# Twin items of queries and keys on 128 partitions, a planned first phase, and fp32 transposes back

## The chip, the cores and the metric

The kernel runs on one core of a Trainium2 chip. The metric is the device time of one execution in microseconds (us). A profiled execution also has a span, from its first to its last instruction, which is some 1.8 us shorter than its time (457.6 and 459.36 us for the kernel before). All times of places inside the kernel are counted from the start of the span. Only one run of each kernel has its trace kept, so a place read from a trace is that of one execution.

Engines are named as the profile names them. PE is TensorE's matmuls and PEld its weight loads. DVE is VectorE, ACT is ScalarE, POOL is GpSimd, and SP is the engine that issues most transfers. SBUF and PSUM are the two memories in which the kernel lays its tiles, on up to 128 partitions. PE's results lie in PSUM.

## The reference

```python
# q, k, v: (8, 12, 448, 64) float32; tau = 0.1; w_in: (768, 2048); w_out: (2048, 768)
q_n = q / (norm(q, axis=-1, keepdims=True) + 1e-6)
k_n = k / (norm(k, axis=-1, keepdims=True) + 1e-6)
scores = q_n @ k_n.transpose(0, 1, 3, 2) / tau
attn = softmax(scores)                       # with 1e-9 in the denominator
x = (attn @ v).transpose(0, 2, 1, 3).reshape(3584, 768)
h = x @ w_in
g = h * clip(h + 3, 0, 6) / 6
out = g @ w_out
```

There are 96 heads, worked in 48 pairs, and six pairs make a batch. The first matrix product (`w_in`) of a batch needs all six of its pairs. The second (`w_out`) follows it.

## The kernel before

For each pair the queries and keys are loaded as float32, squared, summed, and scaled to bf16 unit vectors. PE transposes them and makes the scores, ACT takes the exps, and PE multiplies by the values. DVE divides by the sums, PE transposes back, and DVE copies the result to `xT`. Between these, "units" of the two matrix products of the batch before keep PE full: 16 units of the first product and 6 or 8 of the second per batch. In the first six pairs there are no units yet.

One load brings the queries of two pairs into all 128 partitions. The two heads of a pair lie on partitions 0 to 63 and 64 to 127. One transpose gives a pair's queries on 64 partitions and its keys on the others, and this kernel moves each on by copies of 64 partitions (five a pair, of 189 to 393 ns):

```python
    def load_qk(d, first=0, n_pairs=2, e0=nc.sync, e1=nc.sync):
        ...
        for n, (t, e) in enumerate(((q, e0), (k, e1))):
            e.dma_start(
                out=raw_of[d][:, first : first + n_pairs, n, :],
                in_=t[b, h : h + 2 * n_pairs].rearrange("(i g) (p c) d -> (g p) i (c d)", g=2, c=7),
            )
    ...
        copy(qT[lo, :], z[lo, :, 0, :])          # in transposes(): five copies of 64 partitions
        ...
    def back(i, bank):                           # the way back, in bf16
        for j in range(4):
            nc.tensor.transpose(Z[:, q_cols(b, j)], on[:, j, :, :], ident[:, :])
        nc.vector.tensor_copy(out=xT[...][:, hp, ...], in_=Z[:, 0:S])
```

The steady loop, from pair 6 on, issues units around the way back of the pair before:

```python
        n = 1 if i % HP == 0 else 2
        issue(us[:n])
        prepare(i, 2)
        if i > HP:
            back(i - 1, next_bank())
        issue(us[n:])
```

Six PSUM banks are shared by scores, transposes and units (the "ring" of `M0`, `M1`, `Y`, `Z`, `M2`, `M3`).

## Time and profile before

| | before |
|---|---|
| time, median of 3 runs | 458.64 us (458.5 to 459.07) |
| span of the profiled run, its clock | 457.6 us, 0.992 |
| first exp of pair 0 | 11.62 us |
| first scores of pair 6, the first with units | 37.91 us |
| first scores of pair 12, from where PE is full | 83.97 us |

Each digit is the busy share of one of 40 slices of 11.4 us, in tenths.

```profile
DMA  8999996505325144234244253244152001021022
```

### The profile page before, as it was taken

What the parts mean: (1) busy time and instruction counts of PE and PEld (TensorE: products, weight loads), DVE (VectorE), ACT (ScalarE), POOL (GpSimd) and SP (SyncE); (2) the same over time, 40 slices, a digit from 0 to 9 for tenths busy, and PEclk for the clock granted to TensorE, in tenths of its full rate; (3) what the DMA queues carried; (4) which work ended last, traced back from release to release, by engine and by line L of the source; (5) the groups of instructions that cost most, each with busy time, mean ns of one, the idle gap of its engine ahead of it and who ended that gap; (6) DMA issues with size and microseconds to landing.
All of it is one profiled execution on the core that took longest, in us unless ns stands there. A gap on an engine that the chain in (4) does not pass through costs nothing.

```text
span 457.6 us, 9825 instructions
## 1 busy us (share of the span) xinstructions
PE 432.5 (95%) x3872; PEld 260.5 (57%) x3872; DVE 277.0 (61%) x610; ACT 268.3 (59%) x584; POOL 187.2 (41%) x158
## 2 busy tenths in 40 slices
PE   1779799999999999999999999999999999999996
PEld 0455455556666666656666565656666566665553
DVE  6787487767654775775764766776674655414500
ACT  4797588567635665766754576576573657503410
POOL 4996865446144263364261561562460630000000
PEclk9999799999999999999999999999999999999999
DMA  8999996505325144234244253244152001021022
GB/s 279 222 246 259 250 214 173 145 13 157 112 63 172 23 135 140 72 103 139 64 109 144 51 157 111 62 139 129 31 155 52 19 19 36 19 69 36 1 72 69
DMA packets 41167, 50.98 MB, mean 111 GB/s; under 512 B 4256, under 2 KB 41120, under 8 KB 41120
## 3 DMA queue, kind: packets, MB, share of 16 engines
q1 hardware_dynamic: 35504, 43.50, 33.7%
q0 software_dynamic: 5248, 6.29, 8.2%
q8 instruction: 30, 0.49, 0.5%
q10 hardware_dynamic: 368, 0.56, 0.4%
q14 instruction: 17, 0.14, 0.1%
HBM read 45.61 MB, written 11.01 MB: 124 GB/s over the span
## 4 chain that ended last, share of the span: by engine, by line
PE 85%; ACT 5%; DVE 3%; issue 2%; DMA 2%; POOL 2%; SPq 0%; POOLq 0%; ACTq 0%; DVEq 0%
PE M L297 21%; PE M L323 20%; PE PV L258 9%; PE Y L323 6%; PE Z L297 5%; PE Z L323 5%; PE Y L297 5%; PE M L207 5%; ACT at L214 3%; PE M L170 2%; PE M L285 2%; DVE gT L308 1%; PE Y L207 1%; ACT u L305 1%; DMA vr<-in_v_dram 1%
## 5 line engine op out<-in xcount | busy, mean ns | idle before, releaser
L152 POOL TENSOR_TENSOR nrm<-raw,r 128x896 bf16<-128x896 f32 x47 | 79.3, 1688 | 184.1 <-ACT r L145 154.2
L323 PEld LDWEIGHTS <-gT 128*128 128x128 bf16 x896 | 87.3, 98 | 59.1 <-DVE gT L308 0.6
L214 ACT ACTIVATE at<-M 128x448 bf16<-128x448 f32 x197 | 94.8, 568 | 27.9 <-PE M L207 15.9
L297 PE MATMUL M<-xT,w_in_sb 128*128 128x448 bf16 x516 | 108.1, 355 | 0.0
L297 PEld LDWEIGHTS <-w_in_sb 128*128 128x128 bf16 x768 | 73.6, 98 | 59.0 <-issue 2.4
L323 PE MATMUL M<-w_out_sb,gT 128*128 128x384 bf16 x576 | 98.5, 326 | 0.2 <-DVE gT L308 0.2
L121 POOL TENSOR_TENSOR sq<-raw 128x896 f32<-128x896 f32 (+3 forms) x47 | 75.0, 1597 | 4.8 <-DMA raw<-in_k_dram 2.8
L308 DVE SCALAR_TENSOR_TENSOR gT<-u,M 128x448 bf16<-128x448 bf16 x86 | 52.5, 619 | 36.4 <-ACT u L305 36.1
L305 ACT ACTIVATE u<-M,half_bias 128x448 bf16<-128x448 f32 x86 | 53.9, 637 | 35.2 <-PE M L297 34.4
L258 PEld LDWEIGHTS <-at 128*128 128x128 bf16 x1344 | 54.1, 98 | 34.3 <-issue 23.4
L258 PE MATMUL PV<-vx,at 128*128 128x65 bf16 (+1 forms) x1344 | 65.2, 199 | 4.2 <-ACT at L214 3.6
L129 DVE TENSOR_REDUCE n<-sq 128x14 f32<-128x896 f32 x48 | 51.8, 1079 | 3.5 <-POOL sq L121 3.2
L207 PE MATMUL M<-qT,kz 64*128 64x448 bf16 (+1 forms) x197 | 41.9, 353 | 4.0 <-DVE gT L308 2.0
L348 ACT COPY o<-M 128x384 f32<-128x384 f32 x17 | 8.1, 478 | 48.3 <-PE M L323 48.3
L272 DVE RECIPROCAL rc<-PV 128x8 f32<-128x8 f32 x48 | 9.9, 206 | 41.4 <-PE PV L258 41.2
L170 PEld LDWEIGHTS <-nrm 128*128 128x128 bf16 x336 | 23.1, 101 | 20.8 <-DVE nrm L152 8.4
L273 DVE TENSOR_TENSOR on<-PV,rc 128x512 bf16<-128x512 f32 x48 | 33.2, 692 | 1.7
L214 ACT ACTIVATE at<-Z 128x448 bf16<-128x448 f32 x48 | 27.2, 566 | 11.2 <-PE M L207 10.9
L323 PE MATMUL Y<-w_out_sb,gT 128*128 128x384 bf16 x176 | 30.4, 326 | 0.0
L297 PE MATMUL Z<-xT,w_in_sb 128*128 128x448 bf16 x132 | 29.7, 363 | 0.0
L160 POOL CAST vx<-vr 128x512 bf16<-128x512 f32 x48 | 29.3, 611 | 0.8 <-DMA vr<-in_v_dram 0.8
L350 DVE COPY o<-M 128x384 f32<-128x384 f32 x18 | 10.0, 558 | 32.1 <-PE M L323 28.7
(58 smaller groups left out, 422.7 us busy)
## 6 DMA issues: line engine op xcount, KB each, us to landing
out_dram<-o SPq DMA_DIRECT2D x111, 96.0 KB, 2.2
raw<-in_q_dram SPq DMA_DIRECT2D x23, 448.0 KB, 4.1
raw<-in_k_dram SPq DMA_DIRECT2D x23, 448.0 KB, 5.2
vr<-in_v_dram SPq DMA_DIRECT2D x48, 128.0 KB, 4.8
vr<-in_v_dram SPq DMA_DIRECT2D x48, 96.0 KB, 4.6
w_in_sb<-in_moe_w_in_dram POOLq DMA_DIRECT2D x4, 768.0 KB, 12.9
w_out_sb<-in_moe_w_out_dram POOLq DMA_DIRECT2D x4, 768.0 KB, 10.1
raw<-in_q_dram SPq DMA_DIRECT2D x2, 224.0 KB, 3.7
```

Of the source, the lines that this page charges most:

```text
L121: eng.tensor_tensor(out=sq[:, :, n_act:7, :], in0=a[:, :, n_act:7, :], in1=a[:, :, n_act:7, :], op=ALU.mult)
L129: nc.vector.tensor_reduce(out=n2_of[first][:, i - first, :], in_=sq_of.pop(i)[:, :, :, :].rearrange("p n c d -> p (n c) d"), axis=AX.X, op ...
L152: eng.tensor_tensor(out=nrm[:, :, :, :].rearrange("p c n d -> p n c d"), in0=raw_pair(i), in1=r_of.pop(i).rearrange("p (n c) -> p n c", n= ...
L170: nc.tensor.transpose(Z[:, t * 128 : (t + 1) * 128], nrm[:, c, :, :], ident[:, :])
L207: nc.tensor.matmul(out, kt[rows, c0 : c0 + 128], qT[rows, :], start=True, stop=True)
L214: nc.scalar.activation(out=out, in_=in_, func=AF.Exp, scale=inv_tau)
L258: nc.tensor.matmul(o, at[:, n, q_cols(i // HP, j)], mv, start=(name == "A0" and j % 2 == 0), stop=last, skip_group_check=True,)
L273: nc.vector.tensor_tensor(out=on[:, :, :, :].rearrange("p (b j) h d -> p b (j h) d", b=2), in0=pv4[:, :, :, 0:D], in1=rc[:, :, :].to_broad ...
L297: nc.tensor.matmul(ps[:, 0:S], w_in_sb[:, cc, fc * 128 : (fc + 1) * 128], x[:, cc, c0 : c0 + S], start=(cc == 0), stop=(cc == CC - 1),)
L305: nc.scalar.activation(out=u[:, :], in_=ps[:, 0:S], func=AF.Relu, bias=half_bias[:, :], scale=1.0 / 6.0)
L308: nc.vector.scalar_tensor_tensor(out=g[:, fc, c0 : c0 + S], in0=u[:, :], scalar=1.0, in1=ps[:, 0:S], op0=ALU.min, op1=ALU.mult,)
L323: nc.tensor.matmul(ps[:, 0:MH], lhs, w_out_sb[:, fc, m * MH : (m + 1) * MH], start=(fc == 0), stop=(fc == FCN - 1),)
```

## The change

The change has four intents: fewer DVE copies per pair, a first phase without holes, PE kept at full speed at the start (before, seven transposes take 0.93 us at 8.44 us and 0.56 at 22.94), and units of the two products evenly spread.

1. A **twin item** is the queries (or the keys) of two pairs. One head of each pair is in each half of the partitions, so that one transpose gives both heads of a pair on 128 partitions. Each item is loaded by two DMAs, one into each half of the partitions.
2. The first 12 pairs are issued from a written list of operations (`PLAN`) that all engines follow in order, with 20 dummy matmuls (`D`) that keep PE busy.
3. The way back is a matmul with the identity into float32 PSUM, in place of a bf16 transpose. Its last piece is 64 columns instead of 128.
4. Units are regrouped, and a left-over first-product unit of a batch is carried into the next pair (`carry`).

The core of the diff, with cuts marked by dots:

```diff
+PLAN = [
+    "LQ.0.sa D.12 LQ.1.sa SQ.0.a.0.1 SQ.0.v.1.4 SQ.0.p.5.2 RE.0 LQ.2 SQ.1.a.0.5 SQ.1.v.5.2 NO.0.0 RE.1 LQ.3",
+    "SQ.2.p.2.5 NM.0.v NO.0.1 SQ.2.a.0.2 TR.0.Z LQ.4 NM.1.p SQ.3.a.0.7 D.5 RE.2 CQ.1.a RE.3 CQ.0.a LV.0",
+    ...
-        for n, (t, e) in enumerate(((q, e0), (k, e1))):
-            e.dma_start(
-                out=raw_of[d][:, first : first + n_pairs, n, :],
-                in_=t[b, h : h + 2 * n_pairs].rearrange("(i g) (p c) d -> (g p) i (c d)", g=2, c=7),
-            )
+        f = (q, k)[j % 2][b, h : h + 4].rearrange("(i g) (p c) d -> i p g (c d)", g=2, c=7)
+        for i in range(2):
+            engines[e[i % len(e)]].dma_start(out=r[64 * i : 64 * i + 64], in_=f[i])
 ...
-            nc.tensor.transpose(Z[:, q_cols(b, j)], on[:, j, :, :], ident[:, :])
+            c, e = q_cols(i // HP, j), slice(0, 128)
+            if j == 3:
+                c, e = (slice(0, SR), slice(0, SR)) if i // HP % 2 else (slice(SM, S), slice(SR, 128))
+            nc.tensor.matmul(z[:, c], on[:, j, :, :], ident[:, e], start=True, stop=True)
 ...
-            u = first[3 * n : 3 * n + 3]
-            ...
+            u = [first.pop(0) for _ in range(n_first[n])]
+            units[(b + 1) * HP + n] = carry + u + lag[: n_lag[n]]
+            carry, lag = [], lag[n_lag[n] :]
+        carry, lag = first, second(b)
```

In the plan, `LQ` loads an item, `SQ`, `RE`, `NO` and `NM` square, reduce, take norms and scale it, and `TR` transposes. `CQ`, `CK` and `CS` are the copies, and `VC` is the cast of the values to bf16. The letter behind an operation is its engine (`v` DVE, `p` POOL, `a` ACT).

## The prediction

> **What bounds the kernel now.** I read the page's busy shares first, then the slices, then stretches, then PE's waits.
>
> ```profile
> PE 432.5 (95%) x3872; PEld 260.5 (57%) x3872; DVE 277.0 (61%) x610; ACT 268.3 (59%) x584; POOL 187.2 (41%) x158
> ...
> PE   1779799999999999999999999999999999999996
> ...
> PEclk9999799999999999999999999999999999999999
> ```
>
> PE bounds the whole from slice 6 on (a slice is 11.4 us). Before that it has holes, and in slice 5 its clock drops. The stretches are cut where pair 0's exps start (11.6), where pair 6 starts (38.7), and in the middle of pair 12 (88.6):
>
> ```profile
> core 0: us, PE busy (x) PEld busy (x) DVE busy (x) ACT busy (x) POOL busy (x), PEclk, DMA share, GB/s
> 0.00:11.60 11.60, 2.02 (x11) 0.89 (x11) 7.63 (x30) 5.21 (x13) 5.45 (x12) 1.00 0.89 280
> 11.60:38.70 27.10, 21.98 (x271) 13.82 (x271) 21.76 (x52) 22.54 (x41) 25.48 (x24) 1.00 1.06 239
> 38.70:88.60 49.90, 45.34 (x420) 26.17 (x420) 36.54 (x79) 35.56 (x82) 28.29 (x24) 0.93 0.87 197
> 88.60:400.00 311.40, 310.07 (x2847) 189.06 (x2844) 195.69 (x425) 191.31 (x426) 127.97 (x100) 1.00 0.33 92
> ```
>
> In the first six pairs POOL is the full engine (25.48 of 27.10 us); from 88.6 on PE is (310.07 of 311.40). Busy PE is not PE at its rate, so I take the rate from starts in the timeline's steady part: pair 18's work on PE, without its way back, runs from 262.20 to 264.64 (2.44 us), the way back takes 0.23, a unit of the first matrix product 1.135 (264.64 to 266.91 is two), a unit of the second 2.60. A pair is 2.67. Pair 12's scores start at 83.97; done by then are 12 pairs (32.0), 16 first units (18.2) and one second unit (2.6): 52.8 us of warm work. So **31 us of PE time are lost before pair 12**, and almost nothing after. This is all that the change can win from.
>
> The waits name the same places: 8.4 us for the first `nrm`, then exps, and one throttle (in the timeline the first-product units at 50.3 and 52.5 take 2.2 us each instead of 1.13).
>
> ```profile
> PE Z L170 <- DVE nrm L152: 8.4, 1, 8.4
> PE PV L258 <- ACT at L214: 3.6, 5, 1.6
> PE M L207 <- DVE gT L308: 2.0, 9, 0.3
> PE M L207 <- ACT at L214: 1.7, 1, 1.7
> ```
>
> [...]seven transposes take 0.93 us at 8.44 and 19.02, 0.56 at 22.94, and the clock is halved again after the holes before 48.25. [...]189 ns for 448 columns; the trace has 6 in 1.135 us, 189. [...]
>
> ```profile
> L286 DVE COPY xT<-M 128x448 bf16<-128x448 bf16 x32 | 12.3, 385 | 5.9 <-PE M L285 5.9
> L350 DVE COPY o<-M 128x384 f32<-128x384 f32 x18 | 10.0, 558 | 32.1 <-PE M L323 28.7 <-ACT r L145 3.4
> ```
>
> **The change part by part.** Below I use start-to-start intervals of operations that did not wait (shorter than their durations, since they overlap): ACT exp of 448 0.423, of 896 0.81, relu 0.517, a group of norms 1.04, a copy of 448 some 0.42; DVE reduce 1.005, product 0.535, reciprocal and scale 0.85, bf16 copy of 448 0.30; POOL scale or square 1.63, cast 0.57.
>
> 1. Twin items. PE's transposes stay 7 a pair. DVE's five copies of 64 partitions per pair (two of 378, then 393, 356, 189 ns: 1.69 us) become one of 448, one of 384 and two of 64 columns (385 + 356 + 2 x 190 = 1.12). That saves 0.57 us a pair, 27 us of DVE in all, nearly all beside a full PE: worth nothing by itself after pair 12, worth slack before.
>
> 2. The back transposes in fp32. The fourth has 64 columns in place of 128: at most 56 - 27 ns, 0.03 us a pair, some 0.8 us over the 36 pairs of the PE-bound part. DVE's copy to `xT` grows from 385 to an estimated 625 ns (558 plus 64 more columns[...]): +0.24 us, 11 us in all, hidden except in point 5.
>
> 3. The start. The first scores now need a q and a k item, of two pairs each. The last of these four loads should land near 5.6 us, as the second pair's did. Then by hand: squares, reduce of q 6.1, of k 7.6, norms 8.6, POOL's scale of k 10.3, transposes 11.1 (warm: 17 dummy matmuls keep PE busy), copies 11.6, and ACT still has a group of norms to 12.2. First exp near 12.2 against 11.62: 0.6 later, but with two pairs ready and a warm array.
>
> 4. The plan. From the first exp to the last of pair 5 I count on ACT 18 x 0.81 + 6 x 0.43 + 3 x 1.04 of norms + 1.3 of copies = 21.7 us; DVE 19.8; POOL 21.5 (some squares and scales moved away). Before, these took 27.1. At 92% of the fullest engine: 23.6, so 35.8. From there to pair 12: PE 6 x 2.67 + 15 x 1.135 = 33.0; ACT 42 x 0.423 + 15 x 0.517 + 3 x 1.04 + 3.8 of copies and squares = 32.5; DVE 30.2; POOL 24. Three engines nearly equally full and six shared PSUM banks: I take 90%, 36.7. Pair 12's scores then start at **72.5**. At that point this kernel has done one first unit and one second unit less, and seven transposes more, than the kernel before at 83.97, so the equal point before is 83.97 - 1.135 - 2.60 + 0.44 = 80.7. **Gain 8.2 us.** The 90 and 92% are my choice: POOL, full in the first stretch before, reached 94%, alone.
>
> 5. A new wait at each batch's first pair (12, 18, ... 42: six times). The units were regrouped so that the one before the way back is now a first-product unit left over from the older batch; it was a second-product unit. DVE therefore takes that unit's product before the copy to `xT`, and the sixth matmul of the next unit reads just that copy. The instruction order of the changed kernel shows it: that sixth matmul alone waits on DVE. The timeline of before, for a first unit whose matmuls give way to the next operation at 92.06:
>
> ```profile
> 92.06 0.65 PE L258 MATMUL PV<-vx,at 128*128 128x65 bf16 x16
> 92.27 0.63 ACT L305 ACTIVATE u<-M,half_bias 128x448 bf16<-128x448 f32 x1 [0.50 <-PE M L297]
> 92.93 0.62 DVE L308 SCALAR_TENSOR_TENSOR gT<-u,M 128x448 bf16<-128x448 bf16 x1 [0.51 <-ACT u L305]
> ```
>
> So the copy could start 93.47 - 92.06 = 1.41 after the unit's slot and ends at about 2.08 with its 0.62; PE wants it after four transposes and five matmuls, 0.21 + 0.95 = 1.16. The stall is 0.9, more where ACT still works on the seven exps (they run for 3 us from 0.4 us into the pair, the unit ends at 2.9: up to 0.3 later). I take 1.0: **6.0 us lost.** Before, the copy started right after a plain eviction and PE passed without a hole.
>
> 6. Won back in the steady part: before, a pair after one that ended in a first unit waited for its product with its sixth score (0.2 us of idle in the waits view, but ends are modelled: between starts it is some 0.45, since the two scores before it start at 92.85 and about 0.19 later, and it at 93.61), six times after 88.6: 2.7 us. Now all but two iterations end in a second unit: 1.8 us won.
>
> Sum: 458.6 - 8.2 + 6.0 - 1.8 - 0.8 = **453.8 us**.
>
> **The rivals.** (a) The plan's order stalls: engines run in order, and three of them nearly full wait for each other; at 80% in both stretches pair 12 starts at 80.5, and nothing is won: 461. Against it: the plan alternates the engines operation by operation, and evictions are split from their units. (b) The plan is nearly perfect and the start dense: 97%, pair 12 at 68.6, and 450. For it: three engines have slack in the first stretch that POOL did not have. (c) The stall of point 5 does not happen or is half: 451. Against it: the semaphore is in the program. (d) Weights become the wait: their loads are spread over the plan, and took 12.9 us to land; the second and third quarter of `w_in` are issued, by my count, some 10 to 13 us before use. A miss could cost 2 to 4 us, and a PE hole might halve the clock again: 457. For it: the DMA engines' share was over 1.0 up to 60 us; against it: fewer bytes are asked early.
>
> **Range and chances.** The plan's end is uncertain by about 3.5 us, the stalls by 1.5, the rest by 1: 4 us in the square sum, so 449.3 to 457.8 for eight in ten. Faster by over 2% means under 449.5: it needs (b), or half of (b) and (c) together. Slower than 467.8 needs a failure that I see no sign of.
>
> **What would show it.** First exp near 12.2; pair 5's last exp near 36; pair 12's first score near 72.5, with PE above 85% from 36 on and no half clock after 10 us. Six PE waits of about 1 us for DVE's `xT`, 55 us apart or less; their absence refutes point 5. POOL far below 94% between 12 and 36. `xT` copies near 625 ns. The steady period of two batches should be 105 us plus the two stalls. If pair 12 starts after 78 the plan has failed, and the waits in its second half will say on whom.

Cuts in this text are marked. They take out statements on the hardware that no trace of this study shows. No term of the sum is cut: it came to 453.8 us, as it stands. What the traces show in these places:

- The clock. In the trace of before the granted clock is 0.50 from 48 to 54 us, after the holes that the text names. "Warm" is a stretch in which seven transposes take 0.56 us and not 0.93. At 8.44 and 19.02 they took 0.93 although the page's clock reads 1.00 there.
- The copies. The two lines give 385 ns for 448 columns, bf16 from bf16, and 558 ns for 384 columns, fp32 from fp32. The step in point 2 from 558 to 625 ns is the author's estimate. The trace of after gives 617.
- The 56 and 27 ns of point 2. Seven transposes in 0.56 us, the last of them 0.22 long, start some 57 ns apart. From the first matmul of a way back to the next operation it is 0.22 us before (202.83 to 203.05) and 0.20 after (200.75 to 200.95).
- The overlap. An exp of 448 columns lasts 0.55 us where the next one starts 0.42 to 0.43 us after it (264.04, 264.47 and 264.89 in the trace of before).

## More of the kernel before

Runs of one kernel scatter. The kernel before took 456.4 to 456.9 us in the runs whose mean granted clock was 0.999, and 458.1 to 461.1 in those with 0.992 to 0.995.

## The result, and the profile after

The changed kernel took **462.05 us** (median of 4 runs, 461.18 to 462.26), against 458.86 (458.5 to 459.6) for the kernel before in the same rounds. The ratio is 1.0064, with a 95% interval of 1.0045 to 1.0083. A ratio here is the mean time of one kernel's runs over that of the other's of the same rounds, so it is not quite the ratio of the medians quoted. The change costs 0.6%. That is inside the band of 2%, but clear of the noise, and above the predicted range.

The page after, the same rows (slices of 11.5 us):

```profile
PE 433.2 (94%) x3891; PEld 259.9 (56%) x3892; DVE 265.9 (58%) x559; ACT 271.6 (59%) x601; POOL 180.7 (39%) x147
...
PE   4678989999999999999999999999999999999996
...
PEclk9899999999999999999999999999999999999999
DMA  8989999903442443424434324433342001221022
```

DVE has 51 instructions and 11 us less, as intended. The half-clock stretch in slice 5 (0.50 from 48 to 54 us) is gone, but the clock now drops in slice 2 (0.50 from 12 to 15). PE is busier in the first slice, with dummies, and in the fifth. In slices 2, 4 and 6 it is a little less busy than before. The DMA row is full for two more slices than before, although the same 51 MB are moved.

Stretches after, cut at the first exp (16.5), at pair 6's first scores (40.4) and at pair 12's (78.1). The columns are the length, the busy time of each engine with its instructions, the clock, the DMA share and GB/s:

```profile
0.00:16.50 16.50, 9.30 (x35) 3.91 (x36) 9.55 (x32) 7.23 (x19) 9.39 (x13) 0.90 0.91 223
16.50:40.40 23.90, 17.77 (x258) 11.64 (x256) 23.31 (x44) 21.48 (x40) 21.21 (x15) 1.00 0.94 220
40.40:78.10 37.70, 35.43 (x374) 20.72 (x373) 31.13 (x63) 33.85 (x82) 21.97 (x21) 1.00 1.05 220
78.10:460.10 382.00, 370.68 (x3234) 223.67 (x3232) 201.86 (x422) 209.09 (x461) 128.16 (x101) 1.00 0.35 88
```

The last stretch of before, from its pair 12 on:

```profile
84.00:457.60 373.60, 367.77 (x3219) 222.54 (x3217) 214.51 (x459) 209.06 (x460) 127.97 (x100) 1.00 0.31 86
```

So the change gains 83.97 - 78.1 = 5.9 us up to pair 12, and then takes 382.0 - 373.6 = 8.4 us longer to the end. By the prediction's own count 3.3 us of that are work not yet done at pair 12 (1.135 + 2.60 - 0.44). The other 5.1 us are lost time.

PE's waits after, the lines that matter (total us, times, longest):

```profile
PE Z L231 <- DVE nrm L200: 4.3, 1, 4.3
PE M L384 <- DVE xT L239: 4.1, 4, 1.0
...
PE Y L384 <- DVE xT L239: 1.8, 2, 1.0
```

Two things stand out. The six waits for `xT` are there, 5.9 us. And the first scaled item (`nrm`) came late. PE's timeline at the start shows how late:

```profile
2.48 5.30 PE L480 MATMUL Y<-zeros 128*128 128x512 bf16 x12 [2.48 <-DVE vx L530]
12.05 0.93 PE L231 MATMUL Z<-ident,nrm 128*128 128x128 bf16 x7 [4.27 <-DVE nrm L200]
12.77 2.34 PE L480 MATMUL Y<-zeros 128*128 128x512 bf16 x5
14.90 0.76 PE L231 MATMUL Y<-ident,nrm 128*128 128x128 bf16 x7
16.11 0.55 PE L292 MATMUL SC<-qT,kz 64*128 64x448 bf16 x4 [0.45 <-DVE kz L239]
```

The twelve dummies end at 7.78. The first transposes come 4.27 us later, when the granted clock has just dropped (0.95 from 11 to 12 us, 0.50 from 12 to 15): seven of them take 0.93 us, and the five dummies behind them 2.34. The first scores start at 16.11, against 10.34 before.

### The profile page after: what moved, and what is told of

It reads as the page before. It is cut to its first block, busy times and chain, and to the rows that moved or that the text cites. A ratio compares the mean times of both kernels' runs of the same rounds, so it can differ in the third digit from the quotient of the medians.

```text
span 460.1 us, 9885 instructions
## 1 busy us (share of the span) xinstructions
PE 433.2 (94%) x3891; PEld 259.9 (56%) x3892; DVE 265.9 (58%) x559; ACT 271.6 (59%) x601; POOL 180.7 (39%) x147
## 4 chain that ended last, share of the span: by engine, by line
PE 78%; ACT 10%; DMA 5%; DVE 4%; issue 1%; SPq 1%; POOL 1%; DVEq 0%; ACTq 0%
PE M L417 22%; PE M L384 17%; PE PV L334 8%; ACT at L309 7%; PE Z L417 6%; DMA raw<-in_k_dram 5%; PE Z L384 5%; PE Y L384 4%; PE M L292 4%; PE Y L417 4%; PE M L231 2%; ACT u L393 1%; DVE gT L399 1%; PE Y L292 1%; PE Z L292 1%
## 5 line engine op out<-in xcount | busy, mean ns | idle before, releaser
L200 POOL TENSOR_TENSOR nrm<-raw,r 128x896 bf16<-128x896 f32 x45 | 76.9, 1711 | 129.8 <-ACT r L191 129.7
L417 PE MATMUL M<-w_out_sb,gT 128*128 128x384 bf16 x624 | 105.7, 326 | 0.0
L384 PE MATMUL M<-xT,w_in_sb 128*128 128x448 bf16 x486 | 101.6, 352 | 4.1 <-DVE xT L239 4.1
L166 POOL TENSOR_TENSOR sq<-raw 128x896 f32<-128x896 f32 (+5 forms) x46 | 73.4, 1597 | 51.2 <-DMA raw<-in_q_dram 31.8
L399 DVE SCALAR_TENSOR_TENSOR gT<-u,M 128x448 bf16<-128x448 bf16 x81 | 50.3, 621 | 43.4 <-ACT u L393 43.4
L334 PE MATMUL PV<-vx,at 128*128 128x65 bf16 (+1 forms) x1344 | 63.3, 198 | 1.0 <-DVE on L350 1.0
L292 PE MATMUL M<-qT,kz 64*128 64x448 bf16 (+1 forms) x199 | 40.0, 354 | 1.4 <-DVE kz L239 1.4
L309 ACT ACTIVATE at<-Y 128x448 bf16<-128x448 f32 x49 | 27.7, 565 | 16.3 <-PE Z L292 16.3
L384 PE MATMUL Y<-xT,w_in_sb 128*128 128x448 bf16 x144 | 31.5, 352 | 1.8 <-DVE xT L239 1.8
L417 PE MATMUL Z<-w_out_sb,gT 128*128 128x384 bf16 x160 | 27.6, 326 | 0.0
```

The costliest lines, as they stand in the source:

```text
L166: engines[e].tensor_tensor(out=o, in0=i, in1=i, op=ALU.mult)
L200: engines[e].tensor_tensor(out=nrm[:, :, :, :].rearrange("p c g d -> p g c d"), in0=raw_of.pop(j)[:, :, :, :], in1=rs[d % 2][3][:, j % 2, ...
L292: nc.tensor.matmul(o, kt[rows, c0 : c0 + 128], qt[rows, :], start=True, stop=True)
L309: nc.scalar.activation(out=o, in_=x, func=AF.Exp, scale=inv_tau)
L334: nc.tensor.matmul(o, at[:, n, q_cols(i // HP, j)], mv, start=(name == "A0" and j % 2 == 0), stop=last, skip_group_check=True,)
L384: nc.tensor.matmul(ps[:, 0:S], w_in_sb[:, cc, fc * 128 : (fc + 1) * 128], x[:, cc, c0 : c0 + S], start=(cc == 0), stop=(cc == CC - 1),)
```

## The experiments

Theory **L** (loads): the new loads of 64 partitions bring the data late, and the whole prefix with it. Rival **P**: the order of the plan, or its dummies, is at fault. Theory **S** (stalls): the six waits for `xT` cost some 6 us in the steady part. Rival **D**: a delay there is absorbed elsewhere. A third theory, **G**, that a cast on DVE is held up while POOL works, was formed after the first four runs. All twelve kernels gave correct results. Each was timed in five rounds.

### x1_before_half: the kernel before with loads of 64 partitions

```diff
-            e.dma_start(out=raw_of[d][:, first : first + n_pairs, n, :], in_=t[b, ...].rearrange("(i g) (p c) d -> (g p) i (c d)", ...))
+            for g in range(2):
+                e.dma_start(out=raw_of[d][64 * g : 64 * g + 64, first : first + n_pairs, n, :],
+                            in_=t[b, h + g : h + 2 * n_pairs : 2].rearrange("i (p c) d -> p i (c d)", c=7))
```

> The kernel before, with each of its q and k loads (128 partitions) cut into two loads of 64 partitions; nothing else. Theory L (loads to 64 partitions move only some 0.25 MB per us, loads to 128 partitions 0.40, and this made the changed kernel's start late): first exp 2 to 4 us later than 11.6 us, the DMA engines' share stays near 1 beyond 60 us, time 461 to 464 us. Rival P (the late start comes from the plan's own order of operations and its dummy matmuls, not from the loads): time as before, 458.9 within 0.6 us, first exp at 11.6.

Measured: 461.77 us (459.85 to 462.7) against 458.8, ratio 1.0066 [1.0044, 1.0089]. The first scores start at 12.31 (10.34), pair 6 at 41.02 (37.91). The form of the loads alone, in a kernel without a plan, costs the kernel before 3 us. This spoke for L, and its two rates are near those of the traces (394 GB/s in the kernel before from 3 to 7 us, 269 in the changed kernel from 3 to 8). It has a flaw, though: the edit halves the partitions of a load and also doubles the number of loads. Its DMA share between 3 and 8 us is only 0.86. x10 takes this up.

### x2_after_heads: the changed kernel with one load of 128 partitions per item

Heads 0 and 1 of four are paired with 2 and 3 instead of 0 with 1, so that an item is one rectangle in DRAM. The values are loaded to match, and the rows of `w_in` in another order, each quarter in four DMAs.

```diff
-        f = (q, k)[j % 2][b, h : h + 4].rearrange("(i g) (p c) d -> i p g (c d)", g=2, c=7)
-        for i in range(2):
-            engines[e[i % len(e)]].dma_start(out=r[64 * i : 64 * i + 64], in_=f[i])
+        f = (q, k)[j % 2][b, h : h + 4].rearrange("(g i) (p c) d -> (i p) g (c d)", g=2, c=7)
+        engines[e[j % len(e)]].dma_start(out=r, in_=f)
```

> The changed kernel, with heads paired as 0 with 2 and 1 with 3 of each four, so that the two pairs of an item lie one after the other in memory and an item is one load of 128 partitions (w_in's rows permuted to match, as four smaller loads for each quarter). Theory L: first exp at 12.5 to 13.5 us in place of 16.5, pair 12's scores at 73 to 75 in place of 78.1, DMA share under 0.9 before 60 us, time 457 to 459 us. Rival P: first exp near 16 and time 462 within 1 us.

Measured: **465.11 us** (460.63 to 467.15), ratio 1.0117 [1.007, 1.0164], slower than the changed kernel. The start did what L says, with the same order and the same dummies, so P falls for it: first scores at 12.87, first exp at 13.47. But pair 6 came at 44.61 and pair 12 at 82.59, where 73 to 75 was expected. A wait that was not there before had taken its place. PE's wait, then DVE's and POOL's timeline between 35.5 and 43:

```profile
PE PV L333 <- DVE on L349: 6.0, 2, 5.7
```

```profile
36.14 6.60 DVE L208 CAST vx<-vr 128x512 bf16<-128x512 f32 x1
```

```profile
36.49 1.67 POOL L165 TENSOR_TENSOR sq<-raw 128x896 f32<-128x896 f32 x1
38.13 1.68 POOL L199 TENSOR_TENSOR nrm<-raw,r 128x896 bf16<-128x896 f32 x1
39.78 1.03 POOL L165 TENSOR_TENSOR sq<-raw 128x512 f32<-128x512 f32 x1
40.77 1.68 POOL L199 TENSOR_TENSOR nrm<-raw,r 128x896 bf16<-128x896 f32 x1
```

One cast of the values on DVE took 6.60 us. The same cast takes 1.51 in the changed kernel, and others there take 0.42. It lasted as long as POOL worked without a gap: POOL's last operation ends at 42.45, the cast at 42.74. The cast outlasted four of POOL's instructions, which took no longer than usual (1.68 us for a scale of 896 columns, 1.69 in the kernel before). My expectation of the time was a miss, and theory G came from it. The traced run is one of the four slower ones (463.8 to 467.2). The other two took 460.6 and 461.3, and whether the cast was as long in them isn't known.

### x3_after_cx: the copy to `xT` before the left-over unit's product

```diff
-        do("UU", n)
-        do("BK", i - 1)
-        do("CX", i - 1)
+        if i % HP == 0:
+            do("U"); do("UA"); do("BK", i - 1); do("CX", i - 1); do("UV")
+        else:
+            do("UU", n); do("BK", i - 1); do("CX", i - 1)
```

> The changed kernel, with only this order changed at each batch's first pair from pair 12 on: DVE copies xT before it takes the left-over unit's product. Theory S (the six waits for xT cost their idle time and the hidden drain, 6 x 1.1 us): those waits gone, time 455 to 456.5 us. Rival D (the time moves into another wait, such as the sixth score waiting for the product now taken later): at most 2.5 us won, 459.5 or more, and a new PE wait of about 0.5 to 1 us in those six pairs.

Measured: **455.99 us** (453.54 to 457.9), ratio 0.9941 [0.9908, 0.9974], 6.1 us below the changed kernel by the medians. The six waits are gone, and pair 12 to the end takes 375.2 us in place of 382.0. So the stalls cost 6.8 us, of which the waits view shows 5.9. All later kernels with this order agree (x4, x5, x9, x11 and x12 take 375.1 to 375.5 us from pair 12 on), and x2 and x8, which lack it, take 382.0 and 382.1. S holds, and D falls. The timeline of the changed kernel at pair 12 shows one stall. The sixth matmul of a unit alone waits:

```profile
82.25 1.11 PE L384 MATMUL Y<-xT,w_in_sb 128*128 128x448 bf16 x5
84.14 0.35 PE L384 MATMUL Y<-xT,w_in_sb 128*128 128x448 bf16 x1 [0.77 <-DVE xT L239]
```

### x4_after_both: x2 and x3 together

```diff
+        both edits: load_qk of x2, and the order U, UA, BK, CX, UV of x3
```

> Both edits together. Theories L and S, which act in different stretches and so add: 450 to 453 us, faster than both kernels by over 1.2%. If L is false: 455 to 456.5. If D holds: 455 to 457.

Measured: 456.02 us (455.68 to 460.21), ratio 0.9962 [0.9932, 0.9993]. The cast of 6.6 us is there again, with PE's wait of 5.7. Of the two gains only that of x3 shows. In the traced run the start's gain is eaten by the cast. But that run is the slowest of the six (460.21). The other five took 455.7 to 457.1, so a stall of 5.7 us is not shown for them.

### x5_both_vc6_act: x4 with that one cast on ACT

```diff
-    "... VA.4.3 VC.6.v TR.7.Z ..."
+    "... VA.4.3 VC.6.a TR.7.Z ..."
```

> The fourth run's kernel (one load of 128 partitions per item, xT copied first), with one operation moved: pair 6's cast of v, which took 6.6 us on DVE beside seven POOL operations without a gap, goes to ACT. Theory G ([...]the cast waited for a gap of POOL): ACT's cast takes about 0.5 us, PE's wait of 5.7 us for DVE's scaled output is gone, time 450 to 451.5 us. Rival V (the cast waited for its load of v): ACT's cast comes as late, the wait stays, 455 us or more.

Measured: 455.23 us (454.02 to 457.72), ratio 0.9925 [0.9901, 0.995]. The cast took 0.61 us on ACT, and the wait of 5.7 us is gone. Pair 6 starts at 37.17 and pair 7 at 40.12. That the cast waited for POOL is confirmed, and rival V falls. But the gain is smaller than expected, only 0.8 us below x4 by the medians: pair 12 came only at 76.96. Two new waits took the rest, and POOL spent 3.1 us idle on issuing transfers:

```profile
PE M L232 <- POOL nrm L199: 1.5, 1, 1.5
PE Z L385 <- DMA w_in_sb<-in_moe_w_in_dram: 1.5, 2, 1.1
```

### x6_before_dvecast: the kernel before with all casts on DVE

```diff
-        vcast(j, nc.gpsimd)
+        vcast(j, nc.vector)
```

> The kernel before, with all casts of v on DVE in place of POOL, nothing else. Theory G: among POOL's nearly gapless work before 40 us several casts last 1 to 6 us in place of 0.42, and although POOL has 0.57 us a pair less to do, the first stretch doesn't shorten; time 459 to 464 us. Rival V (no exclusion): casts of 0.4 to 0.5 us throughout, the first stretch, where POOL was the fullest engine, some 3 us shorter, time 455 to 457 us.

Measured: 472.55 us (470.61 to 476.35), ratio 1.0298 [1.0267, 1.0329]. A cast takes 0.42 us alone and 1.39 to 1.87 beside POOL. G holds in another kernel, but no cast reached 6 us here: none took longer than one of POOL's operations (1.69) and the cast itself together. Why the cast of x2 outlasted four of them is open. The time was worse than expected. Part of that shows in the copies to `xT`, which now come late:

```profile
PE M L297 <- DVE xT L286: 4.8, 4, 1.2
PE Y L297 <- DVE xT L286: 2.4, 2, 1.2
```

### x7_after_bf16: the changed kernel with bf16 transposes back

```diff
-            nc.tensor.matmul(z[:, c], on[:, j, :, :], ident[:, e], start=True, stop=True)
+            nc.tensor.transpose(zb[:, q_cols(i // HP, j)], on[:, j, :, :], ident[:, :])
```

> The changed kernel, with the back transposes as they were before (bf16, 128 columns in the fourth too). By my working the copy to xT falls from 0.62 to 0.39 us, so each of the six waits for it shrinks by 0.23 (1.4 us in all), and the wider fourth transposes cost 0.026 x 36 = 0.9: 461 to 462 us, within 1 us of the changed kernel. If the fp32 form were a cause of the loss beyond this: under 460.

Measured: 462.06 us (460.55 to 464.79), ratio 1.0071 [1.0047, 1.0095]. The waits for `xT` shrink from 5.9 to 4.3 us, as the copy is shorter. The 0.026 us of the expectation is what the trace of after shows for 64 columns less on the way back (193 ns a matmul against 219). The time doesn't move. From pair 12 on the traced run is 0.8 us shorter (381.2 against 382.0), but before that PE waited 1.9 us for `w_in`, which it didn't in the changed kernel's trace. The fp32 form is not a cause of a loss that shows here.

### x8_after_nodummy: the changed kernel without dummy matmuls

```diff
-    "LQ.0.sa D.12 LQ.1.sa ... D.5 RE.2 ... D.3 FI.0 ..."
+    "LQ.0.sa LQ.1.sa ... RE.2 ... FI.0 ..."
```

> The changed kernel without its 20 dummy matmuls. If the dummies pay by a warm array: seven transposes of 0.9 us and slow scores up to some 20 us, but since DVE, POOL and loads bind there, only 0 to 1.5 us slower, 462 to 463.5 us. If the dummies were what delayed the start (rival P): first scores 1 us or more earlier than 16.1 and the time under 461.

Measured: 462.37 us (460.25 to 465.93), ratio 1.0077 [1.0045, 1.0109]. The first scores start at 13.81 instead of 16.11. About 1 us of this is not the edit's: the first keys happened to be there at 7.67 instead of 8.65. In x7, with dummies and keys at 7.66, the first scores start at 14.71, so the dummies account for some 0.9. Yet pair 6 starts at 40.39, where the changed kernel had 40.37. The first two groups of seven transposes take 0.93 us each without dummies (0.93 and 0.76 in the changed kernel, 0.56 each in x9 and x12, whose data comes earlier). Dummies bring nothing here and cost nothing that shows. Late first scores by themselves are not the loss. The pairs behind them need their data, and from 3 to 40 us that moved at the same rate (236 and 235 GB/s).

### x9_both_wide: x5 with `w_in` in two halves instead of four quarters

```diff
+            if w > 1:
+                return
-            cols = slice(w * FG, (w + 1) * FG)
+            cols = slice(w * 2 * FG, (w + 1) * 2 * FG)
```

> As x5_both_vc6_act, but w_in is loaded in two halves of 1024 columns (eight DMAs in all) instead of four quarters (sixteen). Theory (part of the start's gain was given back between pairs 7 and 9 because GpSimd issued sixteen split w_in DMAs there and the last quarter came late): GpSimd's issue time before the squares falls from about 3 us to under 2, the second w_in wait of TensorE is gone, pair 12's first scores move from 76.96 to about 75, time 452 to 453.5 us. Rival (something else binds between pairs 7 and 9: [...]the order of the plan): pair 12 stays at 76.5 to 77.5 and the time at 455.2 +- 0.7.

Measured: **452.56 us** (450.88 to 453.18), ratio 0.987 [0.9838, 0.9901]. POOL's 3.1 us of issue and both new waits are gone. Pair 12 starts at 73.64. What x5 gave back was an artefact of my own 16 small loads of `w_in`.

### x10_before_split128: the kernel before with two loads, each over 128 partitions

```diff
+                for i in range(2):
+                    e.dma_start(out=o[:, i, :], in_=x[:, i, :])      # one pair each; the first loads are cut by columns
```

> The kernel before with each load of queries and keys cut into two DMAs as in x1_before_half, but each of the two still reaches all 128 partitions. Theory L (what cost 3 us in x1 was that a load reaches only 64 partitions): 458.9 +- 0.8 us, first scores at 10.3 to 10.8, pair 6 at 37.9 to 38.6. Rival C (the number of DMAs, their fixed cost or their issue, was the cause): first scores at about 12.3, 461 us or more.

Measured: 460.71 us (460.27 to 461.23), ratio 1.005 [1.0023, 1.0077]. The first scores start at 11.83. This is between the two theories, and both expectations miss. Cutting alone costs the kernel before 1.6 us, about half of what x1 lost, so x1 had not shown what I took from it. Stretches from 3 to 8 us of the kernel before, then of x10; the last two columns are the DMA share and GB/s:

```profile
3.00:8.00 5.00, 0.00 (x0) 0.00 (x0) 2.61 (x5) 2.03 (x6) 0.82 (x1) 1.00 1.07 370
```

```profile
3.00:8.00 5.00, 0.00 (x0) 0.00 (x0) 1.90 (x4) 1.94 (x6) 0.00 (x0) 1.00 0.86 248
```

In x10 the DMA engines are partly idle (0.86). The trace shows what held the loads back: with the doubled number, SP waited 2.5 us for an earlier load of queries to land before it issued its seventh. The same wait in x1 is 1.4 us. In the changed kernel the DMA engines are full and still slow, as the next lines show. These are two different losses.

### x11_wide_cut64 and x12_wide_cut128: x9 with two loads per item, of 64 and of 128 partitions

To settle the share of the partitions, both kernels issue the same number of loads of the same size on the same queues.

```diff
-        engines[e[j % len(e)]].dma_start(out=r, in_=f)
+        for i in range(2):      # x11
+            engines[e[i % len(e)]].dma_start(out=r[64 * i : 64 * i + 64], in_=f[64 * i : 64 * i + 64])
+        for g in range(2):      # x12
+            engines[e[g % len(e)]].dma_start(out=r[:, g, :], in_=f[:, g, :])
```

> x9_both_wide with each load of queries and keys cut into two DMAs, each into one half of the partitions: the form of the loads in the kernel after. x10 has shown that cutting loads costs something even where each part reaches all 128 partitions, so this run and x12 have the same number of DMAs on the same queues and differ in the partitions alone. Theory L (the partitions matter): DMA engines fully busy at 240 to 280 GB/s between 3 and 8 us, first scores at 14 to 16 us (12.38 in x9), time 454.5 to 456.5. Rival C (only the number of DMAs matters): as x12 to within 0.5 us in first scores and in time.

> x9_both_wide with each load of queries and keys cut into two DMAs, one for each pair of the item, each of them over all 128 partitions. Theory L: DMA rate between 3 and 8 us above 330 GB/s wherever the DMA engines are busy, first scores at 12.4 to 13.4 us, time 452.3 to 454. Rival C: first scores at 14 us or later and the time at 454.5 or more, as in x11.

Measured: x11 454.0 us (453.13 to 455.72), ratio 0.9892 [0.9868, 0.9916]. x12 took **451.8 us** (449.99 to 452.25), ratio 0.984 [0.9816, 0.9863]. Both are 0.5 us better than the range expected. The first scores start at 14.20 and at 11.97, pair 6 at 39.82 and at 36.66. The same five microseconds as above, of the changed kernel, x11 and x12 in this order:

```profile
3.00:8.00 5.00, 4.78 (x12) 1.39 (x10) 2.07 (x8) 0.31 (x1) 1.12 (x1) 1.00 1.05 269
```

```profile
3.00:8.00 5.00, 4.61 (x12) 1.38 (x10) 2.47 (x10) 1.15 (x3) 1.11 (x1) 1.00 1.07 249
```

```profile
3.00:8.00 5.00, 4.77 (x12) 1.39 (x10) 3.69 (x10) 2.17 (x7) 1.97 (x2) 1.00 1.02 356
```

All three have full DMA engines. Those whose loads reach 64 partitions move 249 to 269 GB/s, the one whose loads reach 128 moves 356. L holds and C falls in this kernel: with the number of loads equal, the partitions are worth 2.2 us of the start and 2.2 us of the median time. No run of x11 is as fast as the slowest of x12. In the two traces the gap grows to 3.7 us at pair 12 (76.77 and 73.03), but x12's trace is of its fastest run. The rate is not all of it: up to 8 us SP needed 0.60 to 0.84 us to issue one of x11's loads and 0.33 to 0.44 for one of x12's, and between 1.5 and 2.0 us x11 moved nothing while x12 moved 100 GB/s. No run separates the slower issue from the lower rate. The ratio of the two rates is 249 / 356 = 0.70, with loads into both halves of the partitions in flight together. What sets it was not shown.

x12 is faster than both kernels, by 1.6% against before. Whether it beats x9 is not settled, since their intervals overlap. They were run at other times.

## Why the prediction was wrong

The predicted time was 453.8 us, and the kernel took 462.05. The terms below are counted in the profiled spans, where the error is 7.3 us. The remaining 0.9 or so lies in the base: the profiled run of before took 459.36 us, and the sum started from the median of 458.64. The prediction named pair 5's last exp. I use pair 6's first scores, which follow it directly.

| step of the prediction | predicted | measured | error, us |
|---|---|---|---|
| 3, first exp | 12.2 | 16.52 | +4.3 |
| 4, from there to pair 6 | 23.6 | 23.9 | +0.3 |
| 4, from there to pair 12 | 36.7 | 37.7 | +1.0 |
| 5, six stalls on `xT` | +6.0 | +6.8 | +0.8 |
| 2 and 6 together | -2.6 | -1.7 | +0.9 |

**Point 3 failed.** Its step "The last of these four loads should land near 5.6 us, as the second pair's did" carried over the rate of the kernel before to loads of another form. The squares of the first keys started at 8.65 us. Those of the second pair before, whose loads were the third and fourth, had started at 5.65. The two lines, before and after:

```profile
5.65 0.63 ACT L117 ACTIVATE sq<-raw 128x512 f32<-128x512 f32 x1 [0.85 <-DMA raw<-in_k_dram]
```

```profile
8.65 0.74 ACT L164 ACTIVATE sq<-raw 128x640 f32<-128x640 f32 x1 [3.19 <-DMA raw<-in_k_dram]
```

By then the DMA engines had moved 1.3 MB before and 1.7 MB after, so it is the rate and also what was moved in between. The diff shows the new form of the loads, and the prediction never weighed it. The trace of before held the sign: its loads of values reach 64 partitions each, and in the stretches where they were landing it moved 266 and 243 GB/s (7 to 9 and 12 to 14 us), against 394 from 3 to 7, where queries and keys landed.

How much of the 4.3 us is the partitions? x11 against x12 shows 2.2 us in the first scores, with everything else equal. The remaining 1.9 us, between the changed kernel and x11, looks like scatter between executions. x3, x7 and x8 load queries and keys exactly as the changed kernel does, and their first keys were squared at 7.47, 7.66 and 7.67 us, x11's at 7.15. The traced run of the changed kernel was the late one. The transposes that came late, and the dummies behind them, ran at a granted clock of 0.50, where those of x12 had 1.00. The five dummies took 2.34 us and not 1.24 as in x12, but x8 shows that this cost no time at the end.

For the same reason the split of the error between the rows of the table belongs to this one trace. With loads of 64 partitions, pair 6 starts at 39.8 to 40.8 us in the changed kernel, x3, x7, x8 and x11, although their first exps range from 14.40 to 16.52. With loads of 128 partitions and no long cast (x5, x9, x12) it starts at 36.7 to 37.3. So the form of the loads shows in the whole stretch up to pair 6 and not only in the first exp.

**Point 4 was right in its sums, in part by chance.** This was the step I trusted least. Its 23.6 us agree with the changed kernel's 23.9 only because the first exp was late there: x8, with its first exp at 14.40, needed 26.0. In x12, whose data comes in time, the first exp is at 12.39 (12.2 predicted for the changed kernel), pair 6 starts 24.3 us later (23.6), and pair 12 another 36.4 us later (36.7), at 73.03 (72.5):

```profile
12.40:36.70 24.30, 17.74 (x259) 11.52 (x256) 22.46 (x45) 22.22 (x43) 24.04 (x19) 1.00 0.94 237
36.70:73.00 36.30, 34.74 (x370) 20.55 (x369) 30.97 (x60) 33.60 (x82) 22.70 (x22) 1.00 0.96 222
73.00:448.20 375.20, 369.77 (x3236) 223.63 (x3232) 202.26 (x422) 209.05 (x461) 128.09 (x101) 1.00 0.34 90
```

The plan of operations keeps its promise once the loads do, but not for the reason given. Point 4 made ACT the fullest engine of the first stretch at 92%. In x12 POOL is full (24.04 of 24.30 us; 21.5 were counted) and ACT is at 91%. Part of POOL's time is 2.7 us of issuing `w_in`, where the changed kernel spends 1.0. The sign "POOL far below 94%" didn't come, then, neither here nor in the changed kernel (21.21 of 23.90, 89%). Nor did "no half clock after 10 us": in the changed kernel the clock was 0.50 from 12 to 15. x12 has one cast moved from DVE to ACT, so this is not the changed kernel's plan to the letter, and its trace is of its fastest run, 1.8 us below its median. x9's trace gives 24.2 and 36.4 us. The 1.0 us by which the changed kernel's second stretch was too long is not explained. Its two slow casts on DVE (1.27 and 1.51 us) lie in the first stretch. Rival (a), a plan that stalls, predicted 461 and is close to the measured time, but for the wrong reason. Its stalls are not there.

**Point 5 was right.** The six waits are where the prediction put them, at 1.0 us each, and 6.8 us in all against 6.0. The form of the copy, 617 ns against an estimated 625, was right too. Rival (c), that the stall would be absent, falls.

**Points 2 and 6** together were worth 1.7 us: 6.8 of stalls less the 5.1 lost. The prediction had 2.6. x7 gives a hint which was too large. From pair 12 on it took 0.8 us less than the changed kernel while the waits for `xT` shrank by 1.6. By this estimate, from one trace each, its wider transposes cost 0.8 as point 2 said, and point 6 was worth 0.9 in place of 1.8.

**Point 1 was right.** It called the saving on DVE worth nothing by itself once PE is full. DVE has 11.1 us less to do (277.0 to 265.9; 27 - 11 = 16 by points 1 and 2), and from pair 12 on the kernel is no faster for it. The missing 5 us are mostly operations that the plan shifts between engines, which point 1 left out. By the lists of DVE's operations, DVE got 8 casts of values (5.6 us), 5 more squares (5.1) and 2 more scales (4.1), and gave 15 copies of queries and keys and 4 of `xT` to ACT.

**Rival (d)**, late weights, did not happen in the changed kernel's trace. But it is close: PE waited 1.9 us for `w_in` in x7 and 1.4 in x8, whose loads are the changed kernel's own. In x5 it waited 1.5 us, by my own edit.

A few small sums of the prediction are off, without effect on this reading: pair 6's scores start at 37.91 and not 38.7, so the stretch that "took 27.1" took 26.3; ACT's first sum is 21.6; 36 times 0.03 is 1.0 and not 0.8; 1.41 + 0.62 is 2.03; and 4 us below 453.8 is 449.8.

## What to carry to other kernels

When a change alters the shape of a load, take its rate from a load of that same shape in the trace, not from the load that it replaces. In this kernel 64-partition loads filled the DMA engines at 249 to 269 GB/s, where 128-partition ones reached 356 to 370. An operation that sits off the critical path still decides what waits behind it: moving one DVE copy ahead of one product gave 6.1 us, more than the whole change cost. And when one experiment changes two things at once, as x1 did with the partitions and the number of loads, run the pair that differs in one of them before believing it.
